# The last batch's output chunks in the order 4, 6, 8, 5, 7, and the final chunk copied in two halves

## The chip, the cores and the metric

The kernel runs on one core of one Trainium2 chip. The metric is the device time of one execution in microseconds (us); the figure for a kernel is the median of its runs. Five engines work side by side, each through its own instructions in order: TensorE (PE, matmuls; its weight loads are shown as PEld), VectorE (DVE), ScalarE (ACT), GpSimd (POOL) and SyncE (SP, which here only issues DMA transfers). ACT can issue DMA transfers too, between its own instructions. An engine waits for another through semaphores. Matmul results land in PSUM, from which ACT or DVE must copy them into SBUF before a DMA can store them to HBM.

## The reference

Eight batches, eight heads, 576 rows, head width 64, model width 512. Two attentions, then a gated projection:

```python
p_packed = sm_attn(p, k, v)               # 32 packed rows per head attend to 576 keys
out = sm_attn(q, p_packed, p_packed)      # 576 queries attend to the 32 packed rows
x = out.transpose(0, 2, 1, 3).reshape(B, S, H * D)
gate_pre = sum(conv_w[k] * xp[:, k:k + S, :] for k in range(5))   # causal, 5 taps
gate = 1 / (1 + exp(-gate_pre))
val = x @ w_val
return gate * val @ w_out                 # 8 x 576 x 512, float32
```

The change touches only the last step, the product with `w_out`, and the way its result leaves the chip.

## The kernel before

Each batch runs through stages: loads, both attentions, the gate (`gate`), the value product (`value`) and the output product (`project`). A stage is a generator that yields after every small piece; the string `ORDER` says which generator takes its next step, so the stages of neighbouring batches are interleaved by hand. Every engine is wrapped by `InOrder`, which makes its instructions stand in exactly the order in which they are recorded. All of them have line 66 in the profile, the line of that helper, so groups are told apart by their tiles: `o` is the PSUM result of the output product, `osb` its copy in SBUF, `out_dram` the output.

`project(b)` works on chunks of 128 rows of the output, 512 columns wide. Two batches have 1152 rows, so nine chunks: an even batch makes chunks 0 to 3, the odd one that follows makes 4 to 8. A chunk is twelve matmuls: four slices of the 512 inner columns (`n4`), three terms each (`gvh*woh`, `gvh*wol`, `gvl*woh`; the operands are split into a high and a low part). Its result fills one PSUM bank. It is copied into an `osb` tile, and the two halves of 64 rows (128 KB each) are stored by two DMAs.

The last batch, 7, is done differently (`if b == B - 1`). Its five chunks are accumulated side by side for the first three slices. Chunks 4 and 5 share one two-bank tile, chunks 6 and 7 another, chunk 8 has a tile of its own:

```python
last = big(f"o_{b}_{n}", "duo")
accs.update({c: last[:, c % 2] for c in range(4 + 2 * n, 6 + 2 * n)})
```

Then chunk after chunk gets the three matmuls of its last slice, a copy by DVE, and two stores, one from SP and one from ACT. Dependencies are kept for whole tiles: a matmul that writes one bank of a two-bank tile waits for a copy that reads the other bank, if that copy stands ahead of it in the program.

After the five chunks come chunks 2 and 3 of batch 6 (twelve matmuls each, a tile of one bank each), copied by ACT and stored by two DMAs of SP. They fill the end: the last tokens of `ORDER` are `o7.21 o6.4 o7 H0 o6 H0 o6 H0`, where `H0` is four PE transposes whose result nobody reads. The piece of `o7` that stands behind `o6.4` issues the stores of the last batch's fifth chunk, so on SP and on ACT these stand behind work of chunk 2.

Of the kernel before, what the change touches and what calls it, by code (L numbers as in the profile page):

```python
# [82 lines left out]
def packed_attention_gated_conv(  # L83
# [30 lines left out]
    pe, act, dve, pool, sp = (  # L114
        InOrder(tc, e) for e in (nc.tensor, nc.scalar, nc.vector, nc.gpsimd, nc.sync)
    )
    B, H, S, D = q.shape
    NP = p.shape[2]
    DM = H * D
# [15 lines left out]
    def tile_of(tag, shape, dt, name, pool=sb):  # L135
        return pool.tile(shape, dt, tag=tag, name=name, bufs=NB.get(tag, 2))

    def big(name, tag="big"):
        return ps.tile([P, 2, 512], F32, tag=tag, name=name, bufs=PSB[tag])
# [4 lines left out]
    def one(name, tag="mid"):  # L144
        return ps.tile([P, 512], F32, tag=tag, name=name, bufs=PSB[tag])

    heads = [slice(NP * hl, NP * hl + NP) for hl in range(4)]
    NW = 2 * NP
# [561 lines left out]
    def product(ops, c, n4):  # L710
        for n, (w, x) in enumerate(((gvh, woh), (gvh, wol), (gvl, woh))):
            pe.matmul(
                ops,
                w[:, n4, c * P : c * P + P],
                x[:, n4, :],
                start=(n4 == n == 0),
                stop=(n4 == NC - 1 and n == 2),
            )

    def project(b):  # L720
        chunks = range(0, 4) if b % 2 == 0 else range(4, 9)
        accs = {}
        if b == B - 1:
            for n in range(2):
                last = big(f"o_{b}_{n}", "duo")
                accs.update({c: last[:, c % 2] for c in range(4 + 2 * n, 6 + 2 * n)})
            accs[8] = one(f"o_{b}_8")
            for n4 in range(NC - 1):
                for c in accs:
                    product(accs[c], c, n4)  # L730
                    if n4 or c not in (4, 6):
                        yield
        for c in chunks:
            ops = accs.get(c)
            if ops is None:
                ops = one(f"o_{b}_{c}")
                for n4 in range(NC - 1):
                    product(ops, c, n4)
            product(ops, c, NC - 1)
            yield  # L740

            if b < B - 2:
                osb = tile_of("osb", [P, DM], F32, f"osb_{b}_{c}")
            else:
                osb = tile_of("m", [P, 2 * NE * D], F32, f"osb_{b}_{c}")[:, :DM]
            if b == B - 1:
                dve.tensor_copy(osb, ops)
            else:
                act.copy(osb, ops)
            yield  # L750
            for n in range(2):
                at, e = divmod(2 * c + n, NE)
                to = out[b // 2 * 2 + at].rearrange("(w e) m -> e w m", e=NE)
                (act if b == B - 1 and n else sp).dma_start(to[e], osb[NW * n : NW * n + NW])
            yield

    streams = {
# [1 line left out]
        "C": conv_weights, "W": value_weights, "J": load_out_weights, "N": out_weights,  # L759
        "k": keys, "a": attn_pack, "q": queries, "p": packed_turned, "c": taps, "s": attn_out,  # L760
        "t": weighted, "h": rounded, "w": packed_values, "g": gate, "v": value, "o": project,
    }
    gens = {}
# [45 lines left out]
```

## Time and profile before

| What | Value |
|---|---|
| Median of three runs | 297.67 us |
| The three runs | 297.34, 297.67, 300.65 us |
| Profiled execution: span from its first to its last instruction | 295.2 us |
| Median less the profiled span: what lies around it | 2.47 us |
| PE busy | 279.6 us, 95% of the span |
| DVE, ACT, POOL busy | 193.3, 141.1, 83.2 us |

The profile is of one execution. Its own time outside the span is not given; the median of the runs stands 2.47 us above it, the fastest run 2.14 us. Times of the trace are counted from the start of the span. Matmuls are pipelined and their ends are modelled, so two successive rows overlap; the distance from one start to the next is the safer reading.

### The profile page before, as it was taken

The page shows a single profiled execution, that of the slowest core. Times are in us where ns is not written, and L with a number is a line of the kernel's source. Part 1 is how long each engine was busy: PE and PEld are TensorE (multiplying, and loading weights), DVE is VectorE, ACT ScalarE, POOL GpSimd, SP SyncE. Part 2 cuts the span into 40 slices and gives each one's busy share as a digit, 9 for nine tenths or more (in the row PEclk, how much of TensorE's full clock was granted, in tenths as well). Part 3 has the DMA queues.
Part 4 walks back from the last instruction along what each step waited for, and adds up shares of the span by engine and source line. Part 5 has one row for each costly group of instructions (what it writes and reads, how often), then busy time and mean ns, then how long its engine had stood idle before and what let it go on. Part 6 is the DMA issues. An engine that isn't in the chain of part 4 may idle for free.

```text
span 295.2 us, 10439 instructions
## 1 busy us (share of the span) xinstructions
PE 279.6 (95%) x4660; PEld 214.0 (72%) x4660; DVE 193.3 (65%) x301; ACT 141.1 (48%) x284; POOL 83.2 (28%) x88
## 2 busy tenths in 40 slices
PE   6698798999998999999999999999999999999975
PEld 6475457777687588776878867777796987788764
DVE  3698798998988996985594745746575362325040
ACT  5665696657554456437622473542345263423001
POOL 3724897563322013151206120030423030000000
PEclk9999999999999999999999999999999999999999
DMA  6999996249690691952705107510310043012154
GB/s 206 386 396 348 313 370 222 64 101 298 216 317 9 165 391 37 274 157 47 270 2 151 40 10 226 147 44 2 73 36 4 13 95 73 2 47 63 36 143 107
DMA packets 23903, 43.55 MB, mean 148 GB/s; under 512 B 5898, under 2 KB 5938, under 8 KB 23858
## 3 DMA queue, kind: packets, MB, share of 16 engines
q1 hardware_dynamic: 23458, 42.23, 46.3%
q8 instruction: 36, 0.59, 0.9%
q10 hardware_dynamic: 400, 0.66, 0.7%
q14 instruction: 9, 0.07, 0.1%
HBM read 33.44 MB, written 9.44 MB: 145 GB/s over the span
## 4 chain that ended last, share of the span: by engine, by line
PE 80%; DMA 6%; ACT 5%; DVE 3%; SPq 2%; issue 1%; POOL 1%; ACTq 0%
PE o L66 34%; PE val L66 17%; PE gate L66 13%; PE s L66 6%; DMA km<-in_k_dram 4%; PE pv L66 3%; PE wp L66 2%; DMA p<-in_p_dram 2%; PE at L66 2%; SPq L66 2%; ACT a L66 1%; DVE wo_words L66 1%; PE ppTt L66 1%; DVE osb L66 1%; ACT wo_top L66 1%
## 5 line engine op out<-in xcount | busy, mean ns | idle before, releaser
L66 PE MATMUL o<-woh,gvh 128*128 128x512 f32 x144 | 58.0, 403 | 1.6 <-DVE osb L66 1.6
L66 PE MATMUL o<-wol,gvh 128*128 128x512 f32 x144 | 56.2, 390 | 0.0
L66 PE MATMUL o<-woh,gvl 128*128 128x512 f32 x144 | 56.2, 390 | 0.0
L66 PE MATMUL gate<-a,ppk 32*64 32x288 f32 x1280 | 44.0, 406 | 0.0
L66 ACT COPY osb<-o 128x512 f32<-128x512 f32 x31 | 18.1, 584 | 44.3 <-PE o L66 17.4
L66 PE MATMUL val<-a2h,wph 128*128 128x288 f32 x128 | 38.9, 304 | 0.0
L66 PE MATMUL val<-a2l,wph 128*128 128x288 f32 x128 | 37.8, 295 | 1.1 <-issue 1.0
L66 ACT CAST gvh<-sig 128x576 fp32r<-128x576 f32 x32 | 21.6, 674 | 34.4 <-DVE sig L66 33.9
L66 POOL TENSOR_TENSOR t<-t,sm 128x576 f32<-128x576 f32 x16 | 19.2, 1198 | 66.6 <-DVE sm L66 55.4
L66 PE MATMUL val<-a2h,wpl 128*128 128x288 f32 x128 | 37.7, 295 | 0.0
L66 PEld LDWEIGHTS gate<-a,ppk 32*64 32x64 f32 x1280 | 27.4, 131 | 13.4 <-issue 3.1
L66 PEld LDWEIGHTS o<-woh,gvh 128*128 128x128 f32 x144 | 27.0, 188 | 12.8 <-issue 3.5
L66 DVE SCALAR_TENSOR_TENSOR sig<-sig,val 128x576 f32<-128x576 f32 x32 | 23.8, 744 | 17.9 <-PE val L66 17.7
L66 DVE TENSOR_TENSOR gvl<-sig,gvh 128x576 fp32r<-128x576 f32 x32 | 24.8, 782 | 15.6 <-ACT gvh L66 15.4
L66 POOL TENSOR_TENSOR t<-t,mx 128x576 f32<-128x576 f32 x16 | 20.4, 1272 | 49.9 <-DVE mx L66 49.8
L66 PEld LDWEIGHTS o<-woh,gvl 128*128 128x128 f32 x144 | 27.0, 188 | 6.0
L66 ACT ACTIVATE sig<-gate 128x576 f32<-128x576 f32 x32 | 19.6, 651 | 23.0 <-PE gate L66 23.0
L66 PEld LDWEIGHTS o<-wol,gvh 128*128 128x128 f32 x144 | 27.1, 188 | 4.7
L66 PEld LDWEIGHTS val<-a2h,wph 128*128 128x128 f32 x128 | 24.0, 188 | 5.4 <-issue 2.5
L66 PEld LDWEIGHTS val<-a2h,wpl 128*128 128x128 f32 x128 | 24.0, 188 | 0.5
L66 PEld LDWEIGHTS val<-a2l,wph 128*128 128x128 f32 x128 | 24.0, 188 | 0.3 <-DVE a2l L66 0.3
L66 POOL TENSOR_TENSOR ppk<-ppd,cwb 128x320 f32<-128x320 f32 x16 | 14.2, 902 | 23.2 <-PE gate L66 15.5
(95 smaller groups left out, 429.4 us busy)
## 6 DMA issues: line engine op xcount, KB each, us to landing
km<-in_k_dram SPq DMA_DIRECT2D x16, 576.0 KB, 6.2
qm<-in_q_dram SPq DMA_DIRECT2D x16, 576.0 KB, 6.3
vm<-in_v_dram SPq DMA_DIRECT2D x16, 576.0 KB, 6.2
out_dram<-osb SPq DMA_DIRECT2D x67, 128.0 KB, 2.4
wo_words<-in_moe_w_out_dram SPq DMA_DIRECT2D x4, 512.0 KB, 6.1
wv_words<-in_moe_w_val_dram SPq DMA_DIRECT2D x4, 512.0 KB, 6.1
p<-in_p_dram SPq DMA_DIRECT2D x12, 64.0 KB, 2.4
out_dram<-osb ACTq DMA_DIRECT2D x5, 128.0 KB, 2.9
```

What stands on the lines that cost most here:

```text
L66: made = getattr(self.engine, op)(*args, **kw)
```

## The change

The last batch finishes its chunks in the order 4, 6, 8, 5, 7 in place of 4, 5, 6, 7, 8. The very last chunk of the program (chunk 3 of batch 6) is copied half by ACT (columns 0 to 255) and half by DVE (256 to 511), and its second store moves from SP's queue to ACT's.

```diff
-        for c in chunks:
+        for c in chunks if b < B - 1 else (4, 6, 8, 5, 7):
...
-            if b == B - 1:
+            last = b == B - 2 and c == 3
+            if last:
+                act.copy(osb[:, : DM // 2], ops[:, : DM // 2])
+                dve.tensor_copy(osb[:, DM // 2 :], ops[:, DM // 2 :])
+            elif b == B - 1:
                 dve.tensor_copy(osb, ops)
             else:
                 act.copy(osb, ops)
...
-                (act if b == B - 1 and n else sp).dma_start(to[e], osb[NW * n : NW * n + NW])
+                (act if n and (last or b == B - 1) else sp).dma_start(to[e], osb[NW * n : NW * n + NW])
```

On PE, at the last slice of the last batch (`o_0` is the tile of chunks 4 and 5, `o_1` that of 6 and 7, `o_8` that of chunk 8; in brackets the engine whose semaphore an instruction waits for):

```order
 L66 MATMUL o_0_4119<-wol,gvh 128x512
 L66 MATMUL o_0_4119<-woh,gvl 128x512
-L66 MATMUL o_0_4119<-woh,gvh 128x512 [waits DVE_49]
-L66 MATMUL o_0_4119<-wol,gvh 128x512
-L66 MATMUL o_0_4119<-woh,gvl 128x512
 L66 MATMUL o_1_4120<-woh,gvh 128x512
-L66 MATMUL o_1_4120<-wol,gvh 128x512
-L66 MATMUL o_1_4120<-woh,gvl 128x512
-L66 MATMUL o_1_4120<-woh,gvh 128x512 [waits DVE_49]
```
```order
 L66 MATMUL o_8_4121<-wol,gvh 128x512
 L66 MATMUL o_8_4121<-woh,gvl 128x512
+L66 MATMUL o_0_4119<-woh,gvh 128x512 [waits DVE_49]
+L66 MATMUL o_0_4119<-wol,gvh 128x512
+L66 MATMUL o_0_4119<-woh,gvl 128x512
+L66 MATMUL o_1_4120<-woh,gvh 128x512 [waits DVE_49]
+L66 MATMUL o_1_4120<-wol,gvh 128x512
+L66 MATMUL o_1_4120<-woh,gvl 128x512
```

Before, the matmuls of chunk 5 stood right behind those of chunk 4, and those of 7 right behind those of 6, each with a wait for DVE. Now the two waiting groups stand behind chunk 8, six matmuls after the group whose copy they wait for.

On DVE, the end of its program, the copies of the last batch's chunks and what is new behind them:

```order
-L66 COPY osb_5_4199<-o_0_4119 128x512 [waits PE_49]
-L66 COPY osb_6_4206<-o_1_4120 128x512 [waits PE_49]
-L66 COPY osb_7_4213<-o_1_4120 128x512 [waits DMAHW7_49,DMAHW0_49,PE_49]
-L66 COPY osb_8_4220<-o_8_4121 128x512 [waits DMAHW7_49,DMAHW0_49,PE_49]
-L804 UNCONDITIONAL_BRANCH
+L66 COPY osb_6_4199<-o_1_4120 128x512 [waits PE_49]
+L66 COPY osb_8_4206<-o_8_4121 128x512 [waits PE_49]
+L66 COPY osb_5_4213<-o_0_4119 128x512 [waits DMAHW7_49,DMAHW0_49,PE_49]
+L66 COPY osb_7_4220<-o_1_4120 128x512 [waits DMAHW7_49,DMAHW0_49,PE_49]
+L66 COPY osb_3_4259<-o_3_4239 128x256 [waits DMAHW5_49,DMAHW6_49,DVE_49,Activation_49]
```

The copies follow the new order of the chunks. The new half copy of the final chunk does not wait for PE; it waits for ACT (Activation).

On ACT, the end of its program:

```order
 L66 COPY osb_2_4235<-o_2_4222 128x512 [waits DMAHW4_49,DMAHW3_49,PE_49]
-L66 DMA out_dram<-osb_8_4220 64x512 [waits DVE_49]
-L66 COPY osb_3_4259<-o_3_4239 128x512 [waits DMAHW6_49,DMAHW5_49,PE_49]
+L66 DMA out_dram<-osb_7_4220 64x512 [waits DVE_49]
+L66 COPY osb_3_4259<-o_3_4239 128x256 [waits DMAHW6_49,DMAHW5_49,PE_49]
+L66 DMA out_dram<-osb_3_4259 64x512 [waits DMAHW7_49,DVE_49]
```

The store that stands behind the copy of chunk 2 is now that of chunk 7, and ACT ends with a store of the final chunk, which waits for DVE. SP's only store of that chunk has the same wait for DVE.

## Rows read from the trace of the kernel before

**Rows 1.** The page: busy times of the engines, and the chain by engine.

```profile
PE 279.6 (95%) x4660; PEld 214.0 (72%) x4660; DVE 193.3 (65%) x301; ACT 141.1 (48%) x284; POOL 83.2 (28%) x88
...
PE 80%; DMA 6%; ACT 5%; DVE 3%; SPq 2%; issue 1%; POOL 1%; ACTq 0%
```

**Rows 2.** The chain in order of time, 279 to 296: start, length, what.

```profile
280.40 0.70 DVE osb L66
...
281.14 0.97 PE o L66 x3
...
282.83 0.00 issue
282.83 0.70 DVE osb L66
...
283.58 7.10 PE o L66 x30
```

**Rows 3.** Timeline of PE, 279.5 to 284: start, length, instruction [idle before <-releaser].

```profile
279.97 0.39 PE L66 MATMUL o<-woh,gvl 128*128 128x512 f32 x1
281.14 0.50 PE L66 MATMUL o<-woh,gvh 128*128 128x512 f32 x1 [0.78 <-DVE osb L66]
281.48 0.39 PE L66 MATMUL o<-wol,gvh 128*128 128x512 f32 x1
...
282.40 0.40 PE L66 MATMUL o<-woh,gvl 128*128 128x512 f32 x1
283.58 0.50 PE L66 MATMUL o<-woh,gvh 128*128 128x512 f32 x1 [0.78 <-DVE osb L66]
283.92 0.40 PE L66 MATMUL o<-wol,gvh 128*128 128x512 f32 x1
```

**Rows 4.** Timeline of PE: chunk 2's first matmul and chunk 3's last, 24 in all.

```profile
285.07 0.39 PE L66 MATMUL o<-woh,gvh 128*128 128x512 f32 x1
...
290.29 0.39 PE L66 MATMUL o<-woh,gvl 128*128 128x512 f32 x1
```

**Rows 5.** Timeline of DVE, 279 to 286: the copies of chunks 5 to 8.

```profile
282.14 1.39 DVE L66 COPY osb<-o 128x512 f32<-128x512 f32 x2 [1.05 <-PE o L66]
284.58 1.38 DVE L66 COPY osb<-o 128x512 f32<-128x512 f32 x2 [1.05 <-PE o L66]
```

**Rows 6.** Timelines of ACT and SP from 289: the final chunk's copy and two stores.

```profile
290.71 0.59 ACT L66 COPY osb<-o 128x512 f32<-128x512 f32 x1 [2.14 <-PE o L66]
291.32 0.47 SPq L66 DMA_DIRECT2D out_dram<-osb  x1
291.84 0.59 SPq L66 DMA_DIRECT2D out_dram<-osb  x1
```

**Rows 7.** Copies out of PSUM by form: count | busy, mean ns | idle before.

```profile
L66 ACT COPY a1t<-at 128x512 f32<-128x512 f32 x16 | 9.1, 583 | 3.0 <-PE at L66 3.0
L66 ACT COPY ppT<-ppTt 128x384 f32<-128x384 f32 x8 | 3.8, 477 | 3.4 <-PE ppTt L66 3.4
L66 ACT COPY a1t<-at 128x128 f32<-128x128 f32 x8 | 2.1, 267 | 0.1
...
L66 DVE TENSOR_TENSOR pp<-pv,sm 128x256 f32<-128x256 f32 x2 | 0.8, 411 | 0.0
```

**Rows 8.** Stores to the output: SP's last two, then ACT's five.

```profile
L66 SPq DMA_DIRECT2D out_dram<-osb x2: 467/528/589, 291.3 to 291.8; - x2
...
DMA to landing us min/median/max: 2.3/2.3/2.4
```
```profile
L66 ACTq DMA_DIRECT2D out_dram<-osb x5: 473/499/692, 281.1 to 288.0; - x5
...
DMA to landing us min/median/max: 2.7/2.9/3.0
```

**Rows 9.** Windows: engines' busy time, then PE clock, DMA share, GB/s.

```profile
282.00:284.00 2.00, 1.22 (x6) 0.70 (x5) 1.38 (x2) 0.00 (x0) 0.00 (x0) 1.00 0.49 132
284.00:286.00 2.00, 2.00 (x11) 1.63 (x10) 1.38 (x2) 0.00 (x0) 0.00 (x0) 1.00 0.87 258
```

## The prediction

> **What bounds the kernel now.** I read the busy times and the chain of waits first. PE is busy for 95% of the span and makes 80% of the chain [rows 1]: whatever PE does not wait for any more comes off the end, and little else does. Then the chain in order of time over the last stretch, the only one that the change touches. There PE's run of output matmuls is broken twice by a DVE copy of 0.70 us, at 280.40 and at 282.83 [rows 2]; after 283.58 PE runs without a gap to the last product. The timeline of PE shows the same two places as matmuls that were idle for 0.78 us until an `osb` copy was done, at 281.14 and 283.58 [rows 3]. By the order of the program these are the first matmuls of chunk 5 and of chunk 7, held by the copies of chunks 4 and 6. Last comes the tail behind PE: the copy of the final chunk at 290.71, its stores issued at 291.32 and 291.84 [rows 6], the second landed 2.4 us after its issue [rows 8], at 294.24, and 0.96 us of closing to the span's end at 295.2.
>
> **The reordering.** In free running an output matmul starts every 0.227 us: 24 matmuls, from 285.07 to 290.29, are 23 steps in 5.22 us [rows 4]. From the last matmul of chunk 4 (279.97, [rows 3]) to the first of chunk 2 (285.07) there are thirteen steps, which at that pace take 2.95 us; they took 5.10. So the two joints cost **2.15 us**. A check from the joints alone: 279.97 to 281.48 is 1.51 us for two steps of 0.45, and 282.40 to 283.92 is 1.52, a loss of 1.06 and 1.07.
>
> Are both waits really covered in the new order? Chunk 4's copy still runs from 280.40 for 0.70 us, to 281.10. PE goes on with chunk 6 at 280.20 and chunk 8 at 280.88, and wants chunk 5's first matmul at 281.56: 0.46 us after that copy ended. Chunk 6 is finished by PE at about 281.1 (last start 280.65, plus the 0.43 from 279.97 to 280.40 that separates a last matmul from its copy), so DVE copies it to 281.8, and chunk 7 wants to start at 282.24: 0.44 us to spare. DVE's later copies take 0.69 us each, two of them back to back in 1.38 us also while PE is running [rows 5, 9], against 0.68 us that PE needs for a group of three. So DVE keeps pace and ends near 283.9, with nobody waiting but the stores. I take the whole 2.15. The bounds are 2.15 and nothing, the latter if the copies slip by more than that half microsecond of cover.
>
> What else moves: the stores of 6, 8, 5 and 7 follow their copies 0.7 us apart in place of gaps up to 1.7 us, on both queues. An issue holds its queue for at most 0.69 us on ACT and 0.59 us on SP [rows 6, 8], so the queues just keep up. They stand in front of ACT's copy of chunk 2, which cannot start before PE ends chunk 2 at about 285.9, when the last of the four issues (due near 283.2) is long past. The fifth chunk's stores stand behind chunk 2's work as before, the chunk being 7 in place of 8. I cost this at nothing; the case where it isn't is a rival.
>
> **The split copy.** DVE's half waits for ACT, as the order shows, not for PE. So the halves run one after the other. ACT copies 128 columns in 0.267 us, 384 in 0.477, 512 in 0.583 [rows 7], about 0.106 for each 128, so 256 columns take about 0.37. DVE's nearest row of 256 columns out of PSUM takes 0.41 [rows 7]. With 0.02 us between two engines (the store follows the copy's end by that much in [rows 6]) the data is ready 0.37 + 0.02 + 0.41 = 0.80 us after the start, where the whole copy took 0.59: **0.21 us later**. Bounds: 0.18 earlier, if the halves ran side by side (0.41 against 0.59), and 0.3 later, with some more for DVE's four waits.
>
> **The second queue.** Before, the last store was issued 0.52 us after the first [rows 6] and landed 2.4 us later: 2.92 us from the first issue. Now both are issued at once. SP's will land in 2.3 us; but ACT's stores, issued at the same time as one of SP's, took 2.7 to 3.0 us, median 2.9 [rows 8]. The nearest of these are those with at least 1.5 us since the store pair ahead, which is the case at the end; 2.7 to 2.9, so I take 2.8: **0.12 us earlier**. Bounds: 0.08 later (3.0) and 0.6 earlier (2.3, SP's figure). The Trainium skill, "DMA: Bandwidth & Descriptors", section "Issuing engines are not separate DMA queues", says that transfers started by several engines share the same DMA engines and interleave, and that starting them from more than one engine saves only the time of issuing. By that rule this term would be an issue saved, 0.5 us, and the forecast would be 0.4 us lower; the rows go further against it, since the half that leaves through ACT lands later than its neighbour.
>
> **The sum.** -2.15 + 0.21 - 0.12 = -2.06 us. The profiled span of 295.2 becomes 293.1. Around the span I leave the 2.47 us by which the median of the runs stands above it: 297.67 - 2.06 = **295.6 us**, 0.7% faster. For this kernel a difference under 1%, 2.98 us, is hard to tell from none, so this counts as within 1%.
>
> **The rivals.**
>
> *The tail shrinks as well.* If the halves do overlap (0.18 earlier) and ACT's store lands in 2.3 us (0.6 earlier), the gain is 2.15 + 0.78 = 2.9 us: 294.7, at the edge of 1%. For it: nothing else is in flight then. Against it: the wait for ACT in the built order, and no ACT store under 2.7 us. The Trainium skill, "PSUM — Partial Sum Buffer", section "PSUM bank collisions raise a hardware error", says that two engines must not be in one bank and the same partitions together, and the final chunk is one bank; no row here shows such an overlap. Chance 7%.
>
> *One joint stays.* If PE and DVE working in step slow each other, so that the copy of 6 ends after 282.24, chunk 7 waits again and up to 1.07 of the gain is lost: 296.7. It decides from 0.44 us of slip on; the copies took 0.69 us under a running PE as under a waiting one [rows 5], which speaks against it. Chance 7%.
>
> *The change doesn't do what it says.* If the waits name a later copy than that of the tile's first chunk (chunk 5 waiting for 8's copy, say, which ends near 282.5), each joint costs about 1 us again: 297.67 + 0.09 = 297.8. The order shows that PE waits for DVE, not for which copy; a wait for the reader of the same tile is what the old order showed, at 0.04 us after its end. Chance 4%.
>
> *Slower: the stores pile up.* From 281.1 on, five chunks leave at 0.7 us apart and two more at PE's pace, seven of 256 KB. The DMA engines moved 258 GB/s at a share of 0.87 [rows 9], about 0.9 us for a chunk at full share; 132 GB/s at a share of 0.49 gives 270 GB/s. If pairs from two queues got in each other's way, the first chunk would land at 284.0 (issue plus ACT's median of 2.9), and the end would be set by six more chunks behind it and 0.96 of closing. That passes 295.2 when a chunk takes 1.7 us, and is slower than before by 1% from 2.2 us; at 2.5 us a chunk the span would be 300.0, the time 302.4. Known rows are at half of that. Chance 3%.
>
> **How the numbers follow.** My forecast, with a tail between 0.6 earlier and 0.5 later, has 79%. The predicted time is 295.6. Its own range by the tail's bounds is 294.9 to 296.1. To it I add the distance of the two nearest runs of before, 0.33 us, downwards to the edge of the first rival (294.8) and upwards until the joint that stays is nearly in (296.6). Left out are the lower end of the first rival, no gain, slower, and part of the joint. Faster by over 1% (below 294.69) is half of the first rival and a few percent for an undersized sum: 8%. Slower by over 1% (above 300.65) is the last rival: 3%. Within 1%: 89%.
>
> **What the profile of the changed kernel would show.** PE starts chunk 5 and chunk 7 0.23 us behind the matmul ahead, with no idle time put down to `osb`; chunk 2's first matmul is near 282.9 and chunk 3's last near 288.1, as against 290.29. ACT's half copy of 0.37 us is followed by DVE's of 0.41, not beside it, and the two stores are issued together near 289.4. ACT's lands 2.7 to 2.9 us later and ends the chain. I am wrong if PE is idle before chunk 5 or 7, if the two halves overlap, or if the last landing is more than half a microsecond off 292.2.

## The result

The changed kernel takes 295.47 us (median of ten runs), against 297.96 us for the kernel before (median of ten). The ratio is 0.9918 with a 95% interval of 0.989 to 0.9945. Timed a second time in another series it was 295.85 against 297.60, ratio 0.9948 (0.9925 to 0.9971). So it is faster by 0.5 to 0.8%, under the 1% named in the prediction (the first interval reaches 1.1%). Forecast were 295.6 us and -2.06 us; the two series measured -2.49 and -1.75 us. One of the ten runs, of 315.31 us at a mean granted clock of 0.853, was a slow one: it is in the median, and the ratios use the other runs.

The profiled execution of the changed kernel took 294.97 us with a span of 293.2: 1.77 us lie around the span. The other runs of either kernel for which both figures are on record have about 1.8 us too (one of before: 297.17 and 295.4). The prediction's 2.47 us, the distance of a median to one profiled span, was too much by 0.7: the profiled execution of before was a quick one. The forecast of the time does not hang on it, since it is the median less 2.06 us.

### The profile page after: what moved, and what is told of

It reads as the page before. It is cut to its first block, busy times and chain, and to the rows that moved or that the text cites. A ratio compares the mean times of both kernels' runs of the same rounds, so it can differ in the third digit from the quotient of the medians.

```text
span 293.2 us, 10442 instructions
## 1 busy us (share of the span) xinstructions
PE 279.0 (95%) x4660; PEld 214.9 (73%) x4660; DVE 192.4 (66%) x302; ACT 140.8 (48%) x284; POOL 83.1 (28%) x88
## 4 chain that ended last, share of the span: by engine, by line
PE 86%; DMA 6%; issue 2%; POOL 1%; DVE 1%; ACT 1%; SPq 1%; POOLq 0%
PE o L66 35%; PE val L66 18%; PE gate L66 14%; PE s L66 8%; PE pv L66 4%; PE wp L66 3%; DMA wv_words<-in_moe_w_val_dram 2%; PE at L66 2%; DMA qm<-in_q_dram 2%; DMA km<-in_k_dram 1%; PE ppTt L66 1%; SPq L66 1%; PE qt L66 1%; PE idle L66 1%; ACT ppT L66 0%
## 5 line engine op out<-in xcount | busy, mean ns | idle before, releaser
L66 PE MATMUL gate<-a,ppk 32*64 32x288 f32 x1280 | 43.2, 406 | 0.0
L66 ACT COPY osb<-o 128x512 f32<-128x512 f32 (+1 forms) x31 | 17.8, 576 | 42.1 <-PE o L66 30.4
```

Source lines behind the costliest of these rows:

```text
L66: made = getattr(self.engine, op)(*args, **kw)
```

## The profile after

The chain of the changed kernel in order of time, 277 to 294 (start, length, what), answers to [rows 2]. Both DVE pieces are gone; PE runs in one piece to its idle transposes.

```profile
276.78 12.02 PE o L66 x53
288.80 0.45 PE idle L66 x4
289.25 0.04 issue
289.29 1.09 PE idle L66 x8
```

The timeline of PE answers to [rows 3, 4]: the last matmul of chunk 4, the first of chunks 6, 8, 5, 7 and 2, and the last of chunk 3. No row has idle time.

```profile
280.25 0.39 PE L66 MATMUL o<-woh,gvl 128*128 128x512 f32 x1
280.47 0.39 PE L66 MATMUL o<-woh,gvh 128*128 128x512 f32 x1
...
281.15 0.39 PE L66 MATMUL o<-woh,gvh 128*128 128x512 f32 x1
...
281.83 0.39 PE L66 MATMUL o<-woh,gvh 128*128 128x512 f32 x1
...
282.51 0.39 PE L66 MATMUL o<-woh,gvh 128*128 128x512 f32 x1
...
283.19 0.39 PE L66 MATMUL o<-woh,gvh 128*128 128x512 f32 x1
...
288.41 0.39 PE L66 MATMUL o<-woh,gvl 128*128 128x512 f32 x1
```

From 280.25 to 283.19 are 2.94 us, where before there were 5.10. DVE, in its timeline, makes five copies in a row and much later the half of the final chunk, for which it was idle until ACT was done:

```profile
280.67 3.41 DVE L66 COPY osb<-o 128x512 f32<-128x512 f32 x5 [7.21 <-PE o L66]
289.24 0.42 DVE L66 COPY osb<-o 128x256 f32<-128x256 f32 x1 [5.16 <-ACT osb L66]
```

ACT's timeline at the end, with its half copy and its store, and SP's store at the same moment, answer to [rows 6]:

```profile
288.83 0.37 ACT L66 COPY osb<-o 128x256 f32<-128x256 f32 x1 [2.14 <-PE o L66]
289.69 0.50 ACTq L66 DMA_DIRECT2D out_dram<-osb  x1
```
```profile
289.69 0.47 SPq L66 DMA_DIRECT2D out_dram<-osb  x1
```

ACT's stores answer to [rows 8]: first its four of the burst after the last slice, then its final one. In the burst they landed later than before, up to 3.4 us after the issue against 3.0; the final one took 2.6.

```profile
L66 ACTq DMA_DIRECT2D out_dram<-osb x4: 555/598/697, 281.4 to 283.6; - x4
...
DMA to landing us min/median/max: 2.7/3.3/3.4
```
```profile
L66 ACTq DMA_DIRECT2D out_dram<-osb x1: 499/499/499, 289.7 to 289.7; - x1
...
DMA to landing us min/median/max: 2.6/2.6/2.6
```

The two spans, 295.2 and 293.2, must not be subtracted as they stand. The last matmul of chunk 4 started at 279.97 before and at 280.25 after: the untouched part of the program differs by itself. The experiments are therefore read from that matmul on. In microseconds, by the traces' own times and landing records (differences of times rounded to 0.01 us, so that the last digit can be off by one):

| Kernel | Chunk 4's last matmul to chunk 2's first | Final copy's start to the last landing | Last landing to the end | Chunk 4's last matmul to the end |
|---|---|---|---|---|
| before | 5.10 | 3.50 | 0.99 | 15.23 |
| the change | 2.94 | 3.49 | 0.83 | 12.91 |
| the change, second profile | 2.95 | 3.50 | 0.83 | 12.92 |
| the order alone | 2.95 | 3.50 | 0.99 | 13.08 |
| the tail alone | 5.10 | 3.49 | 0.84 | 15.07 |
| tiles moved, old order | 2.95 | 3.49 | 1.00 | 13.07 |
| one group of cover | 3.36 | 3.49 | 1.00 | 13.49 |
| whole copy, two queues | 2.94 | 3.24 | 0.83 | 12.67 |
| the same, second profile | 2.95 | 3.25 | 0.83 | 12.67 |
| column halves | 2.95 | 2.92 | 1.13 | 12.79 |
| column halves, both queues | 2.95 | 2.60 | 0.89 | 12.24 |

Kernels that share a part agree in it within 0.02 us, so differences of 0.1 us can be read here which the timed runs can't show.

## The experiments

**The order alone.**

```diff
-        for c in chunks:
+        for c in chunks if b < B - 1 else (4, 6, 8, 5, 7):
```

> The order 4, 6, 8, 5, 7 alone; the final chunk is copied whole by ACT and stored twice by SP, as before. Theory (the gain is the two joints on PE): chunk 4's last matmul to chunk 2's first takes 13 steps of 0.227 us, 2.95 us in place of 5.10, and the tail from the final copy's start to the last landing stays at 3.53 us. So 2.15 us less than before, ratio 0.993, about as fast as the whole change. Rival (the tail makes the gain): PE is faster by 2.15 us but the stores, now 0.7 us apart, land later at the end, so that half or more of it is given back; ratio 0.996 or above.

Measured: 295.67 us, ratio 0.9918 (0.989 to 0.9947). On the path 15.23 became 13.08, 2.15 us less, all of it between chunk 4 and chunk 2; the tail stayed. The chain, 279 to 297, is PE alone:

```profile
278.99 10.43 PE o L66 x46
289.42 0.45 PE idle L66 x4
289.87 0.04 issue
289.92 1.09 PE idle L66 x8
```

The first theory holds: the order carries 2.15 of the 2.32 us that the whole change gains on the path, and no landing gives it back.

**The tail alone.** The old order, with the change's other two edits (half copies, `last` in the choice of the queue).

```diff
-        for c in chunks if b < B - 1 else (4, 6, 8, 5, 7):
+        for c in chunks:
```

> The old order 4, 5, 6, 7, 8; only the split final copy and the second queue for its store. Theory: both joints stay (0.78 us idle each), the halves run one after the other (0.37 then 0.42 us), ACT's store lands 2.6 us after its issue, so from the final copy's start to the last landing 3.46 us in place of 3.53: within 0.1 us of before, ratio 1.000. Rival (the tail is worth something by itself): 0.5 us or more off, ratio 0.998 or below, with the halves side by side or the last landing at 2.3 us.

Measured: 297.66 us, ratio 0.9995 (0.9973 to 1.0017). Both joints stand in its waits (279 to 297: who waited for whom, us in total, times, longest), and DVE's half copy waited for ACT's:

```profile
DVE osb L66 <- ACT osb L66: 5.2, 1, 5.2
...
PE o L66 <- DVE osb L66: 1.6, 2, 0.8
```

From the final copy's start to the last landing nothing changed, 3.49 against 3.50. The path was still 0.16 us shorter, 15.07 against 15.23, by what follows the last landing. The tail edits are worth that and no more; the time can't show it.

**Tiles moved.** Chunks finish in the old order, 4, 5, 6, 7, 8, with the old tail; only which chunk shares a two-bank tile with which is changed.

```diff
-            for n in range(2):
-                last = big(f"o_{b}_{n}", "duo")
-                accs.update({c: last[:, c % 2] for c in range(4 + 2 * n, 6 + 2 * n)})
-            accs[8] = one(f"o_{b}_8")
+            o0, o1 = two(f"o_{b}")
+            accs = {4: o0[:, 0], 5: o1[:, 0], 6: one(f"o_{b}_6"), 7: o0[:, 1], 8: o1[:, 1]}
```

> The chunks finish in the old order 4, 5, 6, 7, 8, with the old tail, but the two-bank tiles are shared by chunks 4 and 7 and by 5 and 8, and chunk 6 has the tile of its own. Theory (PE waits because a copy of the same tile stands two groups too close, whichever bank it reads): no idle time of PE at the last slice, 13 steps in 2.95 us, 2.15 us less than before, ratio 0.993, as with the order alone. Rival (what counts is the order in which chunks are finished, copied and stored, or DVE's pace): PE waits for copies as before, ratio 0.998 to 1.000.

Measured: 295.45 us, ratio 0.9913 (0.9881 to 0.9946); path 13.07, as with the order alone. It follows that the order of the chunks is not what matters. A matmul waits for a copy of its tile, though the copy reads the other bank, and two groups between the two users of a tile are the cure, whether the order or the tiles put them there.

**One group of cover.** The order 4, 6, 5, 7, 8, old tail.

```diff
-        for c in chunks:
+        for c in chunks if b < B - 1 else (4, 6, 5, 7, 8):
```

> The chunks finish in the order 4, 6, 5, 7, 8, with the old tail: one group of three matmuls stands between a chunk and the one that shares its tile, not two. Theory (what decides is whether the copy, ended 1.13 us after the chunk's last matmul starts, is over when the next group of the same tile wants to start): chunk 5 wants to start after 0.91 us and starts after 1.17, plus 0.11 for the step behind it; chunk 7 then finds its copy done. From chunk 4's last matmul to chunk 2's first 3.3 us, against 2.95 with two groups and 5.10 before. Rival (a group of another tile in between frees PE altogether): 2.95 us. Rival (a wait for DVE costs the same wherever it stands): 4.0 us or more.

Measured in a single run: 295.5 us; the trace decides here, not the time. Its timeline of PE shows the last matmuls of chunks 4 and 6, the first two of chunk 5, and the first of 2:

```profile
280.22 0.39 PE L66 MATMUL o<-woh,gvl 128*128 128x512 f32 x1
...
280.90 0.39 PE L66 MATMUL o<-woh,gvl 128*128 128x512 f32 x1
281.40 0.50 PE L66 MATMUL o<-woh,gvh 128*128 128x512 f32 x1
281.74 0.39 PE L66 MATMUL o<-wol,gvh 128*128 128x512 f32 x1
...
283.58 0.39 PE L66 MATMUL o<-woh,gvh 128*128 128x512 f32 x1
```

PE was released 1.18 us after chunk 4's last matmul had started (280.22 to 281.40, by the end of that chunk's copy; 1.17 in the kernel before), and one group covers only 0.91 of it. PE lost 0.50 + 0.34 - 0.45 = 0.39 us once, and nothing before chunk 7: 3.36 in place of 2.95, where 3.3 was expected. Both rivals, 2.95 and 4.0, fall. Two groups put seven steps of 0.227 us there, 1.59 us, which is 0.4 more than the release takes; with one group less the wait is back.

**Whole copy, two queues.** The new order; the final chunk copied by ACT alone, its stores from SP and ACT.

```diff
-                (act if b == B - 1 and n else sp).dma_start(to[e], osb[NW * n : NW * n + NW])
+                (act if n and (b == B - 1 or b == B - 2 and c == 3) else sp).dma_start(to[e], osb[NW * n : NW * n + NW])
```

> The new order; the final chunk is copied whole by ACT (0.59 us), and its two stores leave by SP and ACT. Theory (the split costs, the second queue gives): stores are issued 0.61 us after the copy's start in place of 0.86, ACT's lands 2.6 to 2.8 us later, so the tail is 3.2 to 3.4 us: 0.1 to 0.25 us less than the whole change, 0.1 to 0.3 less than the order alone. Ratio to before 0.992. Rival (the split gives): the tail is longer than the whole change's 3.46 us.

Measured: 296.39 us, ratio 0.993 (0.9899 to 0.9962). On the path it is 0.24 us better than the change: 12.67 against 12.91. ACT's timeline shows the whole copy of 0.59 and the store 0.61 us after its start, where the split copy had let it go after 0.86:

```profile
291.31 0.59 ACT L66 COPY osb<-o 128x512 f32<-128x512 f32 x1 [2.13 <-PE o L66]
291.92 0.50 ACTq L66 DMA_DIRECT2D out_dram<-osb  x1
```

Its median was above the change's all the same, so both were run again side by side.

> The whole change once more, beside the next kernel on the same chip. Theory: ratio to before 0.992; 12.95 us from chunk 4's last matmul to the end of the span, 3.46 us from the final copy's start to the last landing, as in its first profile.

> The new order, the final chunk copied whole by ACT and stored from two queues, timed once more beside the whole change. Theory (its first median of 296.4 us came from the stretch before the change, which all kernels share): 12.7 us from chunk 4's last matmul to the end, 0.25 us less than the whole change, ratio to before 0.991, not apart from the whole change by more than the intervals. Rival (something in it slows the kernel elsewhere): its median stays 0.5 us or more above that of the whole change.

Measured: the change 295.85 us, ratio 0.9948 (0.9925 to 0.9971); the whole copy 295.60 us, ratio 0.9932 (0.9908 to 0.9956). The paths repeated to 0.01 us, 12.92 and 12.67. The median of 296.39 did not: that rival falls. The two kernels can't be told apart by their times.

**Column halves.** The new order; the final chunk in two PSUM banks of 256 columns, each half copied into its own tile and stored apart. The edit, shortened:

```diff
+            if b == B - 2 and c == 3:
+                half = DM // 2
+                parts = [one(f"o_{b}_3a")[:, :half], big(f"o_{b}_3b", "duo")[:, 0, :half]]
+                for i, to in enumerate(parts):
+                    # twelve matmuls into `to`, of 256 columns from half * i on
...
+                for i, of in enumerate(parts):
+                    osb = tile_of("m", [P, 2 * NE * D], F32, f"osb_{b}_3{i}")[:, :half]
+                    (act.copy if i else dve.tensor_copy)(osb, of)
...
+                        (act if i and n else sp).dma_start(...)  # half the columns of 64 rows
```

> The new order; the final chunk is computed as two halves of 256 columns in two PSUM banks (24 matmuls in place of 12), each copied into a tile of its own and stored apart (two stores of 64 KB): DVE copies the first half and SP stores it while PE is on the second, ACT copies the second, SP and ACT store it. Theory (the tail behind PE is a copy, an issue and a landing, and is shortened by having less left at the end): copy 0.37 us, issue at once, landing at most 2.6 us, 3.0 us from the last copy's start to the last landing, against 3.46 in the whole change; PE takes 0.2 to 0.5 us more for 24 shorter matmuls. From chunk 4's last matmul to the end 12.4 to 12.9 us, against 12.95 in the whole change and 15.23 before; ratio to before 0.991 to 0.992. Rival (shorter matmuls or smaller packets cost more than that): 13.0 us or more.

Measured: 295.30 us, ratio 0.9917 (0.9888 to 0.9946). From the last copy's start to the last landing 2.92 us, path 12.79: inside what was expected, but not better than the whole copy. The chain, 285 to 297, shows that 24 shorter matmuls took 2.87 us where twelve take 2.72 (12 steps of 0.227):

```profile
286.23 1.43 PE o_3a L66 x12
287.67 1.44 PE o_3b L66 x12
```

What was left was SP. Its three stores of the halves left one behind the other in its timeline (three rows merged, then the last alone), the last at 290.02, though ACT's store of the other 64 rows of the same half had been issued at 289.55:

```profile
288.74 1.83 SPq L66 DMA_DIRECT2D out_dram<-osb  x3
...
290.02 0.55 SPq L66 DMA_DIRECT2D out_dram<-osb  x1
```

**Column halves, both queues.** The same with one word less, so that ACT issues the second store of each half.

```diff
-                        (act if i and n else sp).dma_start(
+                        (act if n else sp).dma_start(
```

> The column halves again, with the second store of the first half moved from SP to ACT. In the first form SP had three issues of 0.55 us in a row, so the last store left SP 0.45 us after its data was ready and landed last. Theory (SP's issues were the tail): the last two stores leave together at 0.41 us behind the last copy's start and land 2.2 to 2.3 us later, 2.7 us in all against 2.92; 12.5 us from chunk 4's last matmul to the end of the span, against 12.80, 12.91 in the whole change and 12.67 with the whole copy from two queues. Ratio to before 0.991. Rival (the landing of the halves is bound by the DMA engines, not by SP's issues): 12.8 us again.

Measured: 294.68 us against 298.79 in that series, ratio 0.9884 (0.9847 to 0.9921). The path is 12.24 us, 0.67 less than the change. ACT's timeline shows the store of the first half issued before the second half's copy, while PE was still at work:

```profile
288.48 0.48 ACTq L66 DMA_DIRECT2D out_dram<-osb  x1
289.46 0.37 ACT L66 COPY osb<-o_3b 128x256 f32<-128x256 f32 x1 [2.29 <-PE o_3b L66]
289.86 0.50 ACTq L66 DMA_DIRECT2D out_dram<-osb  x1
```

The rival (bound by the DMA engines) falls: the last landing came 2.60 us after the last copy's start, not 2.92. The path came out under the expected 12.5: of the 0.55 us against the first form, 0.32 are in the landing and 0.24 in the closing behind it, which the expectation did not speak of. This version beats both kernels by its path. By the ratio alone it is clear of the kernel before; against the change the intervals overlap.

## Why the prediction was right

Its mechanism was right and carried nearly all of the gain. The three signs of being wrong stayed away: PE was not idle before chunk 5 or 7, the halves did not overlap, and the last landing, at 292.32, was near 292.2. That 295.47 us lies so close to 295.6 is partly luck: the forecast started from a median of before of 297.67, the series of the result has 297.96, and the gain by the path was 0.26 us larger than told.

**The joints, -2.15 us: right.** 5.10 became 2.94 or 2.95 in all profiles with two groups between, 2.15 or 2.16 less. The order alone has just this gain. That the wait is for the tile is shown by moving the tiles. That two groups are cover enough is shown by PE without idle time, and that one is not by its run. Chunk 5 began at 281.83; the copy of 4, begun at 280.67, was over near 281.36, so nearly half a microsecond was to spare, as told.

**DVE's pace: right.** Five copies took 3.41 us, 0.68 each, as PE needs for a group.

**Stores at no cost: right, with less reserve than told.** They piled up a little: ACT's landed up to 3.4 us after their issue and SP's up to 2.8, against 3.0 and 2.3 before. It was over by the stores of chunk 2, and the final landing took 3.50 us from the copy's start with the order alone as before it. So the rival of the pile-up had a real mechanism, but it cost single stores about half a microsecond and the end nothing.

**The split, +0.21: right.** The halves ran one after the other, 0.37 and 0.42 us with 0.04 between; the stores left 0.86 us after the copy's start in place of 0.61, 0.25 later. The Trainium skill, "PSUM — Partial Sum Buffer", section "PSUM bank collisions raise a hardware error", forbids two engines in one bank and the same partitions at once; the trace agrees in that the halves of one bank did not overlap, the kernel's wait seeing to it. What the wait came from, the bank or the shared output tile, was not separated.

**The second queue, -0.12: the size was off.** The last landing came 2.63 us after the common issue, not 2.8, against 2.88 from the first issue before (told as 2.92). With the whole copy this edit alone took the tail from 3.50 to 3.24: 0.26 us. The rows chosen for it were stores of a burst; the last one had nothing else in flight but SP's store of the same moment. The Trainium skill, "DMA: Bandwidth & Descriptors", section "Issuing engines are not separate DMA queues", gives only the time of issuing for a second queue, 0.5 us here. Measured is half of that, since the store that leaves through ACT lands 0.3 us after SP's (2.6 and 2.3). ACT's queue by itself is not the slower one: its store of the fifth chunk, issued alone at 286.12 in the changed kernel, landed 2.28 us later.

**The tail together, +0.09 forecast: -0.01 to the last landing, and -0.16 behind it.** The closing after the last landing was taken as fixed at 0.96 (0.99 by the trace's landing record). It was 0.83 with the final stores on two queues and 0.99 to 1.00 with both on SP; the last section says why. So the sum was -2.32 on the path (15.23 to 12.91) where -2.06 was told: a term was missing and another undersized, both to the good.

One bound of the range was summed wrongly: from 297.67 - 2.15, a tail up to 0.5 us later gives 296.0, not 296.1. The forecast does not rest on it.

## What to carry to other kernels

A wait for a copy can come from the tile that two results share, even where they lie in different banks. Read how long the release takes from the last matmul's start (here 1.17 us) and put that much other work between the users of one tile, by order or by placement; less brings the wait back. A split of the last copy over two engines gained nothing while the halves shared a bank and an output tile (it cost 0.25 us). It gained when each half had its own bank and tile, the first half left before the last matmuls were done, and the stores of both halves were shared out over two queues.

## What the hardware showed that was not expected

The time before the changed stretch varies more than the change is worth. The last matmul of chunk 4 started anywhere from 279.97 to 282.72 us in profiles of programs whose work ahead of it is the same. The start goes with the mean of TensorE's granted clock: 279.97 and 280.01 in the two profiles with 0.999 to 1.000, 280.22 to 280.69 in the four with 0.993 or 0.994, 280.72 to 282.72 in the five with 0.987 or 0.988. The stretches of lower clock lie in the first 40 us. The profile of before has none; that of the changed kernel has 0.50, the lower level of 1.2 GHz, from shortly before 33 to beyond 36 us. PE had done little before the clock fell and was busy throughout before it rose. Windows of the changed kernel (start and end, length, busy time of PE, PEld, DVE, ACT and POOL, granted clock, DMA share, GB/s):

```profile
30.00:31.00 1.00, 0.13 (x2) 0.00 (x0) 0.90 (x2) 0.00 (x0) 0.68 (x1) 1.00 1.06 168
31.00:32.00 1.00, 0.00 (x0) 0.00 (x0) 0.00 (x0) 0.49 (x1) 0.86 (x3) 1.00 1.19 240
32.00:33.00 1.00, 0.28 (x2) 0.14 (x2) 0.75 (x1) 1.00 (x3) 1.00 (x1) 0.96 1.05 266
33.00:34.00 1.00, 1.00 (x22) 0.47 (x27) 0.45 (x2) 0.92 (x3) 1.00 (x2) 0.50 1.07 355
34.00:35.00 1.00, 1.00 (x24) 0.20 (x8) 0.75 (x1) 0.49 (x2) 0.86 (x3) 0.50 1.01 383
35.00:36.00 1.00, 1.00 (x42) 0.92 (x35) 0.96 (x3) 0.00 (x0) 0.69 (x1) 0.50 1.09 395
36.00:37.00 1.00, 0.81 (x6) 0.55 (x4) 1.00 (x3) 0.37 (x1) 0.83 (x1) 0.83 1.07 402
37.00:38.00 1.00, 0.73 (x12) 0.57 (x20) 1.00 (x4) 1.00 (x5) 0.86 (x3) 1.00 0.99 380
```

That the clock is the cause is not shown, and it does not explain all of the spread: the profile with 282.72 and one with 280.95 both have a mean of 0.988. Most of the first one's excess arose in one place. PE was idle there for 1.77 us before a group of `pv` matmuls, and the profile names no releaser (timeline of PE in the whole copy's first profile, 87 to 91):

```profile
89.78 0.83 PE L66 MATMUL pv<-vm,a1t 64*32 64x64 f32 x62 [1.77 <-issue]
```

What held it stays open.

The closing behind the last landing was 0.83, 0.89, 0.99 or 1.13 us, and the traces show what decides. SP ends with a row of instructions that wait for semaphores, about 0.06 us from one to the next when nothing is left to wait for. From the end of that row to the end of the span it is 0.75 us in the kernel before, in the changed kernel and with both forms of the column halves. What differs is how much of the row still stands behind the last landing: 0.08 us in the changed kernel, 0.15 with the halves on both queues, 0.25 before, 0.38 with the column halves, where the last landing released the first wait of six. So the -0.16 us behind the landing came because ACT's store, which now lands last, is waited for at the end of the row.
